# Attention chunks on quarter arrays for every unit, and weight sums in buffers of their own, stored one set late in program order

## The chip, the cores and the metric

The kernel runs on one core of one Trainium2 chip. The metric is the device time of one execution, in microseconds (us). Engine names are those of the profile: PE is TensorE's matmuls and PEld its weight loads, DVE is VectorE, ACT ScalarE, POOL GpSimd, SP SyncE (which here issues every DMA).

## What is computed

Chunked attention, whose output goes through a gated two-layer network, all in float32:

```python
# q, k, v: (8, 8, 576, 64); chunks of 64 along the sequence, 9 of them per (batch, head)
scores = (q_c @ k_c.T) / 8                     # 64 x 64 per chunk
attn   = softmax(scores, axis=-1)
x      = (attn @ v_c)                          # laid out as (4608 tokens, 512)
out    = (sigmoid(x @ w_gate) * (x @ w_val)) @ w_out      # 512 -> 1536 -> 512
```

The three weight matrices reach the chip as 64-bit floats and are rebuilt there as a high and a low part. Each large product takes three passes (high x high, high x low, low x high).

## The kernel before

**Blocks, steps, units.** The tokens are cut into nine blocks of 512 (`m`), the 1536 hidden columns into twelve slices of 128 (`f`). Blocks 0 to 2 take a plain path: a step (`m`, `f`) is 24 matmuls `up` (L315), a sigmoid and a product on ACT and DVE, and 12 matmuls `down` (L341) into four accumulators. Blocks 3 to 8 go in three pairs (`n`) through a Strassen-like scheme: seven products `cx`, `cy`, `cz` (L475) of combined inputs `xc` with combined weights `wr`, then `acc` (L550). Attention is cut into 36 units of 16 chunks, four units for each block; two neighbouring units are a pair.

**Weights.** In the first block, twelve slices of weights are loaded (`load_weights`, L110), rebuilt on ACT and DVE (`convert_weights`, L131 to L139) and used at once. During blocks 1 and 2 the kernel stores in DRAM what the Strassen part will read back: copies of the weights (`keep_given` L378, `keep_outer` L383) and 24 sets of weight sums made on POOL (`keep_sums` L392 to L402). The Strassen part loads them with `load_group` (L419, L422) and `load_outer` (L436); the first two groups are asked for in block 2, after step 8.

**Buffers of a set of sums.** `a_val` and `a_sum` come from the two buffers `ob`, through which the output rows of a block also go on their way to DRAM (`evacuate`); `a_both` is one buffer, `spare`, which held the last raw weights before.

**Attention.** Units 0 to 7 go one by one: `products` (L177) against a block-diagonal `kbd`, softmax, four transposes on PE (L222), two half-height copies into the block-diagonal `pbd` (L225 and L227 or L229), and `values` (L238). These matmuls contract over 128 rows and have 64 output rows. Units 8 to 35 go in pairs through `tiled_products` (L271) and `tiled_values` (L286), 32 matmuls of 64x64x64 each, on quarters of the array; their transposes are done on DVE (L614) into alternating halves of `pbd`.

**Order.** START and MIDDLE are lists written by hand: L loads a unit, S or s makes its scores, E its softmax, T or t its transposes, A its values, W loads and C converts weights, H is an `up`, D a `down`. What belongs to START the scheduler orders by itself; from MIDDLE on PE keeps program order, and in `rest()` (blocks 1 to 8) PE and DVE do. SP's queue is ordered by the scheduler throughout. In `rest()`, attention is fed between the matmuls by a credit counter (`tick`, `insert`); the attention loop is `flow`.

Of the kernel before, what the change touches and what calls it, by code (L numbers as in the profile page):

```python
# [29 lines left out]
L0 L1 V0 W0o S0 s1 V1 E0 W0u t0 C0.0 E1 L2 t1 L3 C0.1 A0 A1 W1u S2 C0.2 s3 C1.0 H0.0a E2 W1o E3 C1.1  # L30
T2 W2u T3 D V3 L4 V2 C2.0 A2 C1.2 A3 L5 H0.1a H0.0b W3o D W3u C2.1 C3.0 H0.1b D s4 W4u W2o H0.2 C3.2
C2.2 W4o C3.1 C4.0 D W5u E4 C4.1 C5.0 C5.1 H0.3 D s5 C4.2 t4 E5 W6u H0.4 D W7u C6.0 V5 W6o C7.0 C6.1
# [3 lines left out]
C9.0 W8o C8.2 W9o C9.1 W10u A4 A5 H0.8 W10o D C10.0 C9.2 C10.2 W11u H0.9 C10.1 D H0.10 C11.0 C11.1 D  # L36
W11o H0.11 S7 V7 S6 D L9 E6 H1.0a C11.2 D V6 E7 T6 T7 D H1.1a A6 A7 D H1.0b L8 V8 H1.1b V9 D
# [5 lines left out]

FIRST_TILED = 8
# [6 lines left out]
def chunk_attn_moe(ctx: ExitStack, tc: tile.TileContext, q, k, v, w, out):  # L51
# [17 lines left out]
    early = xp.tile([P, 4, 8, D], F32, tag="x", name="early")  # L69
    zeros = early[:, 0, 0].bitcast(mybir.dt.bfloat16)  # L70
# [4 lines left out]
    pbd = [pbd2[:, i] for i in range(2)]  # L75
    for i in range(2):
        eng = nc.gpsimd if i else nc.vector
        eng.memset(kbd[i][0:D, :, 1, :], 0.0)
        eng.memset(kbd[i][D:P, :, 0, :], 0.0)
# [63 lines left out]
    state, both = {}, {}  # L143
    xt, raw = {}, {}

    def load(j):
        m, h, u = units[j]
        g = 2 * m + h
        qt = ap2.tile([P, 2, 256], F32, name="qt")
        kb = kbd[j % 2]  # L150
        nc.sync.dma_start(qt, q[g, u].rearrange("p (a n) -> p a n", a=2))
        if j >= FIRST_TILED:
            kt = kb[:, :, 0, :]
            nc.sync.dma_start(kt, k[g, u].rearrange("p (a n) -> p a n", a=2))
            state[j] = dict(qt=qt, kt=kt)
            return
        for i in range(2):
            s = slice(i * D, (i + 1) * D)
            nc.sync.dma_start(kb[s, :, i, :], k[g, u, s].rearrange("p (a n) -> p a n", a=2))
        state[j] = dict(qt=qt, kb=kb)  # L160
# [6 lines left out]

    def products(j):  # L170
        s = state[j]
        sc = ps_a.tile([P, 512], F32, tag="psa", name="sc")
        for a in range(2):
            for t in range(2):
                for c in ((0, 1), (1, 0))[a * t]:
                    n0 = (2 * t + c) * D
                    nc.tensor.matmul(  # L177
                        sc[c * D:(c + 1) * D, (2 * a + t) * P:(2 * a + t + 1) * P],
                        lhsT=s["qt"][:, a, n0:n0 + D], rhs=s["kb"][:, a, :, n0:n0 + D],
                        start=True, stop=True,  # L180
                    )
        return sc.rearrange("p (g k) -> p g k", k=D)

    def scores(j, on_scalar=False):
        s = state[j]
        scv = products(j)
        mx = sm.tile([P, 8], F32, name="mx")
        nc.vector.reduce_max(out=mx, in_=scv, axis=AX.X)
        if j < 4:
            pr = early[:, j]  # L190
        else:
            if j // 2 not in both:
                both[j // 2] = ap2.tile([P, 2, 8, D], F32, name="pr", bufs=1)
            pr = both[j // 2][:, j % 2]
        s["pr"] = pr
        if not on_scalar:
            nc.vector.tensor_tensor(out=pr, in0=scv, in1=mx.unsqueeze(2).broadcast_to([P, 8, D]), op=ALU.subtract)
            return
        nc.vector.tensor_scalar_mul(out=mx, in0=mx, scalar1=-0.125)
        sums = s["sums"] = sm.tile([P, 8], F32, name="sums")  # L200
        for i in range(8):
            nc.scalar.activation(
                pr[:, i], scv[:, i], AF.Exp, scale=0.125, bias=mx[:, i:i + 1], accum_out=sums[:, i:i + 1])

    def softmax(j):
        pr = state[j]["pr"]
        if "sums" not in state[j]:
            nc.scalar.activation(pr, pr, AF.Exp, scale=0.125)
            sums = sm.tile([P, 8], F32, name="sums")
            nc.vector.reduce_sum(out=sums, in_=pr, axis=AX.X)  # L210
        else:
            sums = state[j]["sums"]
        nc.vector.tensor_scalar_add(out=sums, in0=sums, scalar1=1e-9)
        inv = sm.tile([P, 8], F32, name="inv")
        nc.vector.reciprocal(out=inv, in_=sums)
        nc.vector.tensor_tensor(out=pr, in0=pr, in1=inv.unsqueeze(2).broadcast_to([P, 8, D]), op=ALU.mult)

    def transposes(j, on_scalar=False):
        pr = state[j]["pr"].rearrange("p (x h) k -> p x (h k)", h=2)
        tp = ps_a.tile([P, 512], F32, tag="psa", name="tp")  # L220
        for i in range(4):
            nc.tensor.transpose(tp[:, i * P:(i + 1) * P], pr[:, i, :], ident)  # L222
        tv = tp.rearrange("p (x q) -> p x q", q=D)
        pb = pbd[j % 2]
        nc.scalar.copy(pb[0:D, :, 0, :], tv[0:D])  # L225
        if not on_scalar:
            nc.vector.tensor_copy(pb[D:P, :, 1, :], tv[D:P])  # L227
        else:
            nc.scalar.copy(pb[D:P, :, 1, :], tv[D:P])  # L229

    def values(j):
        m, h, u = units[j]
        s = state.pop(j)
        pb = pbd[j % 2]
        av = ps_a.tile([P, 512], F32, tag="psa", name="av")
        for c in range(4):
            for a in ((0, 1), (1, 0))[c == 3]:
                nc.tensor.matmul(  # L238
                    av[a * D:(a + 1) * D, c * P:(c + 1) * P],
                    lhsT=s["vt"][:, a, c, :], rhs=pb[:, 4 * a + c, :, :],  # L240
                    start=True, stop=True,
                )
        avv = av.rearrange("p (c h q) -> p h c q", h=2, q=D)
        if m >= FIRST_PAIR:
            n, half = divmod(m - FIRST_PAIR, 2)
            if (n, u) not in raw:
                raw[n, u] = xp.tile([P, 2, 2, TB], F32, tag="x", name="raw")
            dst = raw[n, u][:, :, half, h * 256:(h + 1) * 256]
            nc.scalar.copy(dst.rearrange("p h (c q) -> p h c q", q=D), avv)
            return  # L250
        if h == 0:
            xt[m, u] = xp.tile([P, 2, 2, TB], F32R, tag="x", name="xt")
        x = xt[m, u]
        hi = x[:, 0, :, h * 256:(h + 1) * 256].rearrange("p h (c q) -> p h c q", q=D)
        lo = x[:, 1, :, h * 256:(h + 1) * 256].rearrange("p h (c q) -> p h c q", q=D)
        nc.scalar.copy(hi, avv)  # L256
        nc.vector.tensor_tensor(out=lo, in0=avv, in1=hi.bitcast(F32), op=ALU.subtract)


    def tiled_products(j):  # L260
        sc = [ps_a.tile([P, 512], F32, tag="psa", name="sc") for _ in range(2)]
# [14 lines left out]
    def tiled_values(j, pt):  # L276
        m, h, _ = units[j]
        av = [ps_a.tile([P, 512], F32, tag="psa", name="av") for _ in range(2)]
# [11 lines left out]
        for u in range(2):  # L290
            if m >= FIRST_PAIR:
                n, half = divmod(m - FIRST_PAIR, 2)
                if (n, u) not in raw:
                    raw[n, u] = xp.tile([P, 2, 2, TB], F32, tag="x", name="raw")
            elif h == 0:
                xt[m, u] = xp.tile([P, 2, 2, TB], F32R, tag="x", name="xt")
            for i in range(2):
                src = av[i][:, u * 256:(u + 1) * 256]
                if m >= FIRST_PAIR:
                    nc.scalar.copy(raw[n, u][:, i, half, cols], src)  # L300
                else:
                    hi, lo = (xt[m, u][:, part, i, cols] for part in range(2))
                    nc.scalar.copy(hi, src)
                    nc.vector.tensor_tensor(out=lo, in0=src, in1=hi.bitcast(F32), op=ALU.subtract)
# [140 lines left out]
    def operands(n):  # L445


        low = None
        for i, (name, (u, b), less) in enumerate(MADE):
            at = raw[n, u][:, :, b]  # L450
            if less:
                (u0, b0), (u1, b1) = less
                yield 1.2
# [344 lines left out]
```

## Time and profile before

| | |
|---|---|
| median of 3 runs | 944.46 us (941.83 to 946.08) |
| profiled execution: its own time | 945.38 us |
| profiled execution: span | 943.6 us |
| mean granted TensorE clock | 0.983 |
| busy: PE, PEld, DVE, ACT, POOL | 911.6, 746.7, 604.2, 343.5, 141.7 us |
| DMA | 189.71 MB, mean 201 GB/s |

The profiled execution lasted 1.8 us longer than its span, and 0.9 us longer than the median run. Busy times are unions of intervals on one engine. A granted clock of 1.0 is 2.4 GHz and one of 0.5 is 1.2 GHz; a value between them over a stretch is a mixture of both.

### The profile page before, as it was taken

The numbers are of one execution on the slowest core, as the hardware profiler recorded it, in microseconds if no ns is written. First come the engines' busy times: TensorE is split into PE (matmuls) and PEld (weight loads), VectorE is DVE, ScalarE is ACT, GpSimd is POOL, SyncE is SP. The second block draws the span as 40 slices with busy tenths as digits, with TensorE's granted clock in tenths as the row PEclk, the third lists the DMA queues.
The fourth block names the chain that finished last, engine by engine and source line by source line (L and its number), as shares of the span: only waits on it lengthen the run. The fifth ranks groups of instructions, "written<-read, shape, count | busy, mean of one in ns | idle before, by whom it ended". The sixth has DMA issues, their size and how long they took to land.

```text
span 943.6 us, 14868 instructions
## 1 busy us (share of the span) xinstructions
PE 911.6 (97%) x5856; PEld 746.7 (79%) x5856; DVE 604.2 (64%) x1003; ACT 343.5 (36%) x586; POOL 141.7 (15%) x204
## 2 busy tenths in 40 slices
PE   6899999999999996999999999999999999999998
PEld 4777879888888885788887788888877888888886
DVE  6889875566677664777768675777686335445332
ACT  5989644223234341132342433323324221121222
POOL 1000003990059991000000000000000000000000
PEclk7999999999999997999999999999999999999999
DMA  8788886343143438566575857666565565656661
GB/s 274 236 283 288 282 300 210 131 135 109 53 135 112 135 112 302 188 221 228 189 257 207 283 182 245 199 241 209 198 222 205 186 216 177 205 183 215 221 223 45
DMA packets 80837, 189.71 MB, mean 201 GB/s; under 512 B 7040, under 2 KB 37760, under 8 KB 76160
## 3 DMA queue, kind: packets, MB, share of 16 engines
q1 hardware_dynamic: 80768, 188.77, 58.9%
q8 instruction: 46, 0.75, 0.3%
q14 instruction: 23, 0.19, 0.1%
HBM read 150.99 MB, written 37.75 MB: 200 GB/s over the span
## 4 chain that ended last, share of the span: by engine, by line
PE 73%; DMA 9%; POOL 7%; ACT 4%; DVE 4%; issue 1%; SPq 1%; POOLq 0%; DVEq 0%; ACTq 0%
PE acc L550 19%; PE cy L475 16%; PE cz L475 11%; PE cx L475 11%; PE g L315 9%; PE acc L341 5%; DMA w_raw<-w_in 4%; POOL a_sum L398 2%; POOL a_both L401 2%; POOL a_val L392 2%; DMA sums<-a_both 2%; PE sc L271 1%; PE av L286 1%; POOL a_both L400 1%; DMA wr<-sums 1%
## 5 line engine op out<-in xcount | busy, mean ns | idle before, releaser
L315 PE MATMUL g<-xt,w 128*128 128x512 f32 (+1 forms) x960 | 209.6, 374 | 8.5 <-ACT w L138 3.6
L315 PEld LDWEIGHTS g<-xt,w 128*128 128x128 f32 x960 | 169.4, 191 | 42.7 <-ACT hf L324 3.9
L550 PE MATMUL acc<-wr,hh 128*128 128x512 f32 x576 | 178.0, 390 | 0.0
L475 PE MATMUL cy<-xc,wr 128*128 128x512 f32 x648 | 159.2, 390 | 0.9 <-DVE u L493 0.9
L475 PEld LDWEIGHTS cy<-xc,wr 128*128 128x128 f32 x648 | 121.6, 188 | 26.5 <-DVE u L493 1.3
L550 PEld LDWEIGHTS acc<-wr,hh 128*128 128x128 f32 x576 | 107.9, 188 | 22.4
L475 PE MATMUL cz<-xc,wr 128*128 128x512 f32 x432 | 107.5, 395 | 8.5 <-DMA wr<-sums 8.5
L550 PE MATMUL acc<-wr,hl 128*128 128x512 f32 x288 | 112.7, 391 | 2.9 <-DVE hl L542 2.9
L475 PE MATMUL cx<-xc,wr 128*128 128x512 f32 x432 | 106.1, 391 | 0.0
L475 PEld LDWEIGHTS cz<-xc,wr 128*128 128x128 f32 x432 | 81.4, 190 | 25.9 <-issue 8.9
L614 DVE STREAM_TRANSPOSE pbd<-pr 32x256 f32<-32x256 f32 x224 | 97.6, 436 | 3.9
L542 DVE TENSOR_TENSOR hl<-hid,hh 128x512 fp32r<-128x512 f32 x72 | 49.5, 689 | 76.9 <-ACT hh L540 76.3
L475 PEld LDWEIGHTS cx<-xc,wr 128*128 128x128 f32 x432 | 80.7, 188 | 16.9
L341 PE MATMUL acc<-w,hh 128*128 128x512 f32 x288 | 92.5, 403 | 0.0
L540 ACT CAST hh<-hid 128x512 fp32r<-128x512 f32 x72 | 44.8, 622 | 125.3 <-PE acc L550 102.0
L392 POOL TENSOR_TENSOR a_val<-w 128x256 f32<-128x256 f32 x48 | 38.2, 814 | 206.4 <-DMA out<-ob 204.8
L550 PEld LDWEIGHTS acc<-wr,hl 128*128 128x128 f32 x288 | 54.1, 188 | 16.1 <-DVE hl L542 5.0
L341 PEld LDWEIGHTS acc<-w,hh 128*128 128x128 f32 x288 | 54.0, 192 | 11.6 <-ACT xt L256 0.2
L493 DVE TENSOR_TENSOR u<-cy,s 128x512 f32<-128x512 f32 x36 | 24.8, 688 | 58.2 <-PE cy L475 48.0
L326 DVE TENSOR_TENSOR hf<-g,hf 128x512 f32<-128x512 f32 (+1 forms) x40 | 25.4, 636 | 50.9 <-PE g L315 44.4
L341 PE MATMUL acc<-w,hl 128*128 128x512 f32 x144 | 57.4, 398 | 0.0
L510 DVE TENSOR_TENSOR u<-cy,s 128x512 f32<-128x512 f32 x36 | 24.9, 691 | 46.0 <-PE cy L475 45.9
(109 smaller groups left out, 978.4 us busy)
## 6 DMA issues: line engine op xcount, KB each, us to landing
wr<-sums SPq DMA_DIRECT2D x72, 512.0 KB, 4.6
wr<-outer SPq DMA_DIRECT2D x36, 1024.0 KB, 4.8
w_raw<-w_in SPq DMA_DIRECT2D x36, 512.0 KB, 5.3
wr<-given SPq DMA_DIRECT2D x36, 512.0 KB, 3.7
sums<-a_both SPq DMA_DIRECT2D x24, 512.0 KB, 3.5
qt<-q_in SPq DMA_DIRECT2D x36, 256.0 KB, 4.6
vt<-v_in SPq DMA_DIRECT2D x36, 256.0 KB, 4.4
given<-w SPq DMA_DIRECT2D x36, 256.0 KB, 4.9
```

Source lines behind the costliest of these rows:

```text
L315: nc.tensor.matmul(ps[:, tok], lhsT=wt[f, which][:, wpart, c:c + P], rhs=x[:, part, i, tok], start=n == 0, stop=n == 11)
L326: nc.vector.tensor_tensor(out=hf, in0=pv, in1=hf, op=ALU.mult)
L341: nc.tensor.matmul(acc[m, t], lhsT=hx[:, ts], rhs=wt[f, 2][:, wpart], start=f == 0 and i == 0, stop=f == NF - 1 and i == 2,)
L392: nc.gpsimd.tensor_tensor(out=val[:, 2 * n:2 * n + 2], in0=parts[:, 0], in1=parts[:, 1], op=ALU.add)
L398: nc.gpsimd.tensor_tensor(out=o, in0=x, in1=y, op=op)
L475: nc.tensor.matmul(bank, lhsT=lhs(wpart, c), rhs=x[:, part, c], start=start and k == 0, stop=stop and k == 5, skip_group_check=True)
L493: nc.vector.tensor_tensor(out=u2, in0=y, in1=s1, op=ALU.add)
L510: nc.vector.tensor_tensor(out=u3, in0=y, in1=s1, op=ALU.add)
L540: nc.scalar.copy(hh, h)
L542: nc.vector.tensor_tensor(out=hl, in0=h, in1=hh.bitcast(F32), op=ALU.subtract)
L550: nc.tensor.matmul(acc[m, t], lhsT=hx[:, ts], rhs=wo[f][:, wpart], start=f == 0 and i == 0, stop=f == NF - 1 and i == 2)
L614: nc.vector.transpose(out=pb[dst, :, c, i, :], in_=ps[src, 8 * h:8 * (h + 1), k, :])
```

## The change

All attention units go in pairs over quarter arrays; `products`, `values`, `scores`, `softmax` and `transposes` work on a pair, and `kbd` and `pbd` with their memsets are gone. A pair's transposed scores lie in `pt`, one buffer. For the second pair the scores, and for the first pair the transposes, use accumulator banks of PSUM (`bank`, `aside`). The sums of a set are made in place in a buffer of their own (`sb`), `a_both` alternates between `spare` and a buffer of its own, and the store of a set is issued when the next set has been made. Sets are spread as 1, 1, 2 over three steps through blocks 1 and 2. In `rest()`, SP is put in program order as PE and DVE are.

```diff
-L0 L1 V0 W0o S0 s1 V1 E0 W0u t0 C0.0 E1 L2 t1 L3 C0.1 A0 A1 W1u S2 C0.2 s3 C1.0 H0.0a E2 W1o E3 C1.1
-T2 W2u T3 D V3 L4 V2 C2.0 A2 C1.2 A3 L5 H0.1a ...
+L0 L1 V0 W0o S0 s1 V1 E0 W0u C0.0 E1 L2 t0 t1 L3 C0.1 A0 W1u S2 C0.2 s3 C1.0 H0.0a E2 W1o E3 C1.1
+T2 W2u T3 D V3 L4 V2 C2.0 A2 C1.2 L5 H0.1a ...
...
-    xp = ctx.enter_context(tc.tile_pool(name="xp", bufs=4))
+    xp = ctx.enter_context(tc.tile_pool(name="xp", bufs=2))
+    sb = ctx.enter_context(tc.tile_pool(name="sb", bufs=1))
...
-    kbd = [const.tile([P, 2, 2, 256], F32, name=f"kbd{i}") for i in range(2)]
-    pbd2 = const.tile([P, 2, 8, 2, D], F32, name="pbd")
...
-    for i in range(2):
-        nc.gpsimd.memset(pbd[i][0:D, :, 1, :], 0.0)
-        nc.gpsimd.memset(pbd[i][D:P, :, 0, :], 0.0)
...
     def load(j):
-        kb = kbd[j % 2]
-        nc.sync.dma_start(qt, q[g, u].rearrange("p (a n) -> p a n", a=2))
-        for i in range(2):
-            s = slice(i * D, (i + 1) * D)
-            nc.sync.dma_start(kb[s, :, i, :], k[g, u, s].rearrange("p (a n) -> p a n", a=2))
+        for name, src in (("qt", q), ("kt", k)):
+            t = state[j][name] = ap2.tile([P, 2, 256], F32, name=name)
+            nc.sync.dma_start(t, src[2 * m + h, u].rearrange("p (a n) -> p a n", a=2))
...
+    def bank(name, aside=False):
+        if aside:
+            return ps_o.tile([P, 512], F32, tag="acc", name=name)
+        return ps_a.tile([P, 512], F32, tag="psa", name=name)
+
+    def products(j, aside=False):
+        sc = [bank("sc", aside) for _ in range(2)]
         for u in range(2):
             s = state[j + u]
...
     def scores(j, on_scalar=False):
+        n, i = divmod(j, 2)
+        if n not in pairs:
+            pr = early[:, n] if n < 2 else ap2.tile([P, 8, 2, D], F32, name="pr", bufs=1)
+            pairs[n] = dict(sc=products(2 * n, n == 1), pr=pr, sums={})
...
+    def turned():
+        return ap2.tile([P, 2, 2, 4, D], F32, name="pt", bufs=1)
...
     def transposes(j, on_scalar=False):
+        n, u = divmod(j, 2)
+        s = pairs[n]
+        if u == 0:
+            s["pt"] = turned()
+        tp = bank("tp", n == 0)
+        for g in range(4):
+            nc.tensor.transpose(tp[:, g * P:(g + 1) * P], s["pr"][:, 4 * u + g].rearrange("p i k -> p (i k)"), ident)
+        pt = s["pt"][:, u].rearrange("p a c q -> p (a c q)")
+        if on_scalar:
+            nc.scalar.copy(pt, tp)
+        else:
+            nc.vector.tensor_copy(pt, tp)
...
     def keep_sums(p, which, c):
-        val = mp.tile([P, 4, P], F32, tag="ob", name="a_val")
+        val = sb.tile([P, 4, P], F32, name="a_val")
...
-        sm4 = mp.tile([P, 4, P], F32, tag="ob", name="a_sum")
+        for o, x, y, op in ((3, 2, 3, ALU.add), (2, 0, 2, ALU.subtract), (0, 3, 0, ALU.subtract), (1, 1, 0, ALU.subtract)):
+            nc.gpsimd.tensor_tensor(out=val[:, o], in0=val[:, x], in1=val[:, y], op=op)
+        if c == 0:
+            both = wp.tile([P, 4, 2, P], F32R, tag="spare", name="a_both")
+        else:
+            both = sb.tile([P, 4, 2, P], F32R, name="a_both")
...
-        nc.sync.dma_start(
-            sums[p, which][:, :, c], both.rearrange("p s a n -> p s (a n)").bitcast(F32))
+        return sums[p, which][:, :, c], both.rearrange("p s a n -> p s (a n)").bitcast(F32)
...
-        for t, g, s in ((one, 2, slice(0, 2)), (two, 1, slice(2, 4))):
+        for t, g, s in ((one, 2, slice(0, 4, 3)), (two, 1, slice(1, 3))):
...
-            kept = pr, pbd2[:, j // 2 % 2].rearrange("p (u a c) h q -> p u a (c h) q", u=2, a=2)
+            kept = pr, turned()
...
+    made = []
     def keep(n):
         for _ in range(n):
...
-                keep_sums(p, which, c)
+                made.append(keep_sums(p, which, c))
+            if len(made) > 1 or made and not kept:
+                nc.sync.dma_start(*made.pop(0))
...
-                    keep(1)
-                else:
-                    keep(2)
+                keep(2 if f % 3 == 2 else 1)
+                if m == 2:
                     if f == 8:
                         for which in range(2):
                             load_group(0, 0, which)
...
-        with tc.manual_schedule(engines={mybir.EngineType.DVE}):
+        with tc.manual_schedule(engines={mybir.EngineType.DVE, mybir.EngineType.SP}):
             rest()
```

## Rows read from the trace of the kernel before

**Rows 1.** The page's 40 slices of the span (23.6 us each): granted PE clock, in tenths.

```profile
PEclk7999999999999997999999999999999999999999
```

**Rows 2.** Busy us of the engines in three stretches, granted clock, DMA share, GB/s.

```profile
25.00:45.00 20.00, 15.85 (x126) 13.87 (x125) 17.36 (x37) 19.92 (x47) 0.00 (x0) 0.91 0.71 217
38.00:141.50 103.50, 99.60 (x533) 80.65 (x529) 86.93 (x162) 77.10 (x158) 0.00 (x0) 0.98 0.87 285
141.50:361.70 220.20, 220.18 (x1806) 182.12 (x1802) 143.97 (x237) 77.14 (x117) 137.85 (x192) 1.00 0.39 128
```

**Rows 3.** Waits, whole span: us in total, times, longest us.

```profile
POOL a_val L392 <- DMA out<-ob: 204.8, 2, 151.2
...
PE cz L475 <- DMA wr<-sums: 8.5, 1, 8.5
...
PE g L315 <- ACT hf L324: 2.9, 2, 2.3
```

**Rows 4.** Timeline of POOL, SP's queue and DVE: start us, us, work, idle before.

```profile
269.17 1.99 POOL L392 TENSOR_TENSOR a_val<-w 128x256 f32<-128x256 f32 x2 [53.59 <-DMA out<-ob]
...
356.12 2.15 POOL L401 TENSOR_TENSOR a_both<-a_sum,a_both 128x512 fp32r<-128x512 f32 x1
...
358.30 0.52 SPq L402 DMA_DIRECT2D sums<-a_both  x1
...
361.22 0.59 SPq L422 DMA_DIRECT2D wr<-sums  x1
...
362.78 2.35 DVE L465 TENSOR_TENSOR xc<-raw,xc 128x1024 fp32r<-128x1024 f32 x2
```

**Rows 5.** The chain that ended last, in order: start us, us, work.

```profile
45.01 7.20 DMA w_raw<-w_in
...
61.43 7.35 PE g L315 x24
...
131.16 4.11 DMA w_raw<-w_in
...
174.48 5.44 PE g L315 x24
...
188.08 2.72 PE acc L341 x12
...
362.33 7.76 DMA wr<-sums
370.23 2.90 PE cz L475 x6
373.13 4.33 PE acc L341 x12
...
442.41 1.36 PE cy L475 x6
```

**Rows 6.** Timeline of PE: the products of two units, both ways.

```profile
140.07 1.97 PE L177 MATMUL sc<-kbd,qt 128*64 128x128 f32 x32
...
171.73 1.16 PE L271 MATMUL sc<-kbd,qt 64*64 64x64 f32 x64
```

**Rows 7.** SP's queue, the first and the last stores of weight copies before block 1.

```profile
41.98 0.94 SPq L378 DMA_DIRECT2D given<-w  x2
...
147.43 0.59 SPq L378 DMA_DIRECT2D given<-w  x1
```

**Rows 8.** DMA issues: count, KB each, median us to landing.

```profile
given<-w SPq DMA_DIRECT2D x36, 256.0 KB, 4.9
...
outer<-w SPq DMA_DIRECT2D x12, 512.0 KB, 5.3
```

**Rows 9.** ACT's copies of transposed scores: busy us, mean ns.

```profile
L225 ACT COPY pbd<-tp 64x512 f32<-64x512 f32 x8 | 4.5, 577 | 2.8 <-PE tp L222 2.8
```

**Rows 10.** Groups of DVE's `hl`: 217 to 268 us (POOL idle), then 270 to 357.

```profile
L330 DVE TENSOR_TENSOR hl<-hf,hh 128x512 fp32r<-128x512 f32 x6 | 4.2, 692 | 4.1 <-ACT hh L328 4.1
L330 DVE TENSOR_TENSOR hl<-hf,hh 128x512 fp32r<-128x512 f32 x10 | 9.7, 972 | 7.3 <-ACT hh L328 7.3
```

More of the change, by code (lines that the diff above doesn't have):

```diff
@@ L67, in chunk_attn_moe @@
     ident = const.tile([P, P], F32, name="ident")
-    early = xp.tile([P, 4, 8, D], F32, tag="x", name="early")
-    zeros = early[:, 0, 0].bitcast(mybir.dt.bfloat16)
+    early = xp.tile([P, 2, 8, 2, D], F32, tag="x", name="early")
+    zeros = early[:, 0, 0, 0].bitcast(mybir.dt.bfloat16)
     nc.vector.memset(zeros, 0.0)
-    kbd = [const.tile([P, 2, 2, 256], F32, name=f"kbd{i}") for i in range(2)]
-    pbd2 = const.tile([P, 2, 8, 2, D], F32, name="pbd")
-    pbd = [pbd2[:, i] for i in range(2)]
-    for i in range(2):
-        eng = nc.gpsimd if i else nc.vector
-        eng.memset(kbd[i][0:D, :, 1, :], 0.0)
-        eng.memset(kbd[i][D:P, :, 0, :], 0.0)
-    for i in range(2):
-        nc.gpsimd.memset(pbd[i][0:D, :, 1, :], 0.0)
-        nc.gpsimd.memset(pbd[i][D:P, :, 0, :], 0.0)
     make_identity(nc, ident)
@@ L142, in chunk_attn_moe @@
     units = [(m, h, u) for m in range(NB) for h in range(2) for u in range(2)]
-    state, both = {}, {}
+    state = {}
     xt, raw = {}, {}
@@ L166, in load_values @@
         state[j]["vt"] = vt
[L170 to L190, printed above, removed]
-        else:
[L192 to L257, printed above, removed]
@@ L274, in tiled_products, with scores @@
         return [x.rearrange("p (g k) -> p g k", k=D) for x in sc]
-    def tiled_values(j, pt):
+    pairs = {}
+    def scores(j, on_scalar=False):
+        n, i = divmod(j, 2)
[3 more added lines that the diff above has]
+        s = pairs[n]
+        scv, pr = s["sc"][i], s["pr"][:, :, i]
+        mx = sm.tile([P, 8], F32, name="mx")
+        nc.vector.reduce_max(out=mx, in_=scv, axis=AX.X)
+        if not on_scalar:
+            nc.vector.tensor_tensor(out=pr, in0=scv, in1=mx.unsqueeze(2).broadcast_to([P, 8, D]), op=ALU.subtract)
+            return
+        nc.vector.tensor_scalar_mul(out=mx, in0=mx, scalar1=-0.125)
+        sums = s["sums"][i] = sm.tile([P, 8], F32, name="sums")
+        for g in range(8):
+            nc.scalar.activation(
+                pr[:, g], scv[:, g], AF.Exp, scale=0.125, bias=mx[:, g:g + 1], accum_out=sums[:, g:g + 1])
@@ new lines, in softmax @@
+    def softmax(j):
+        n, i = divmod(j, 2)
+        pr = pairs[n]["pr"][:, :, i]
+        sums = pairs[n]["sums"].get(i)
+        if sums is None:
+            nc.scalar.activation(pr, pr, AF.Exp, scale=0.125)
+            sums = sm.tile([P, 8], F32, name="sums")
+            nc.vector.reduce_sum(out=sums, in_=pr, axis=AX.X)
+        nc.vector.tensor_scalar_add(out=sums, in0=sums, scalar1=1e-9)
+        inv = sm.tile([P, 8], F32, name="inv")
+        nc.vector.reciprocal(out=inv, in_=sums)
+        nc.vector.tensor_tensor(out=pr, in0=pr, in1=inv.unsqueeze(2).broadcast_to([P, 8, D]), op=ALU.mult)
@@ new lines, in turned, with transposes @@
+    def turned():
+        return ap2.tile([P, 2, 2, 4, D], F32, name="pt", bufs=1)
+    def transposes(j, on_scalar=False):
+        n, u = divmod(j, 2)
+        s = pairs[n]
+        if u == 0:
[8 more added lines that the diff above has]
+            nc.vector.tensor_copy(pt, tp)
@@ L277, in tiled_values, with values @@
+    def values(j, pt):
         m, h, _ = units[j]
-        av = [ps_a.tile([P, 512], F32, tag="psa", name="av") for _ in range(2)]
+        av = [bank("av") for _ in range(2)]
         vt = [state.pop(j + u)["vt"] for u in range(2)]
@@ L289, in tiled_values @@
         cols = slice(h * 256, (h + 1) * 256)
-        for u in range(2):
-            if m >= FIRST_PAIR:
[L292 to L304, printed above, removed]
+        n, half = divmod(m - FIRST_PAIR, 2)
+        if m >= FIRST_PAIR:
+            if n not in raw:
+                raw[n] = xp.tile([P, 2, 2, 2, TB], F32, tag="x", name="raw")
+        elif h == 0:
+            xt[m] = xp.tile([P, 2, 2, 2, TB], F32R, tag="x", name="xt")
+        for i in range(2):
+            src = av[i].rearrange("p (u n) -> p u n", u=2)
+            if m >= FIRST_PAIR:
+                nc.scalar.copy(raw[n][:, :, i, half, cols], src)
+            else:
+                hi, lo = (xt[m][:, :, part, i, cols] for part in range(2))
+                nc.scalar.copy(hi, src)
+                nc.vector.tensor_tensor(out=lo, in0=src, in1=hi.bitcast(F32), op=ALU.subtract)
     def up(m, f, which, tok):
@@ L310, in up @@
         for u in range(2):
-            x = xt[m, u]
+            x = xt[m][:, u]
             for i in range(2):
@@ L392, in keep_sums @@
             nc.gpsimd.tensor_tensor(out=val[:, 2 * n:2 * n + 2], in0=parts[:, 0], in1=parts[:, 1], op=ALU.add)
[L393 to L403 removed]
+        for o, x, y, op in ((3, 2, 3, ALU.add), (2, 0, 2, ALU.subtract), (0, 3, 0, ALU.subtract), (1, 1, 0, ALU.subtract)):
+            nc.gpsimd.tensor_tensor(out=val[:, o], in0=val[:, x], in1=val[:, y], op=op)
+        if c == 0:
+            both = wp.tile([P, 4, 2, P], F32R, tag="spare", name="a_both")
+        else:
+            both = sb.tile([P, 4, 2, P], F32R, name="a_both")
+        nc.gpsimd.tensor_copy(both[:, :, 0], val)
+        nc.gpsimd.tensor_tensor(out=both[:, :, 1], in0=val, in1=both[:, :, 0].bitcast(F32), op=ALU.subtract)
+        return sums[p, which][:, :, c], both.rearrange("p s a n -> p s (a n)").bitcast(F32)
     places = [0]
@@ L430, in load_group @@
             1: (of_given(one, 0), "B11"), 2: (of_given(one, 1), "B21"), 6: (of_sums(one, 2), "T2"),
-            5: (of_sums(one, 3), "T1"), 4: (of_given(two, 0), "T4"), 7: (of_sums(two, 1), "T3"),
-            3: (of_sums(two, 2), "B22")}
+            5: (of_sums(one, 3), "T1"), 4: (of_given(two, 0), "T4"), 3: (of_sums(two, 1), "B22"),
+            7: (of_sums(two, 2), "T3")}
     def load_outer(p):
@@ L449, in operands @@
         for i, (name, (u, b), less) in enumerate(MADE):
-            at = raw[n, u][:, :, b]
+            at = raw[n][:, u, :, b]
             if less:
@@ L453, in operands @@
                 yield 1.2
-                nc.vector.tensor_tensor(out=at, in0=raw[n, u0][:, :, b0], in1=raw[n, u1][:, :, b1], op=ALU.subtract)
+                nc.vector.tensor_tensor(out=at, in0=raw[n][:, u0, :, b0], in1=raw[n][:, u1, :, b1], op=ALU.subtract)
             t = wp.tile([P, 2, 2, TB], F32R, tag=f"u{i}", name="xc")
@@ L564, in flow @@
                 yield "S"
-                scv = tiled_products(j)
+                scv = products(j)
                 if j + 2 < 4 * NB:
@@ L582, in flow @@
                 yield "A"
-                tiled_values(j - 2, kept[1])
+                values(j - 2, kept[1])
                 if more:
@@ L671, in run @@
         elif what == "A":
-            values(int(arg))
+            values(int(arg), pairs.pop(int(arg) // 2)["pt"])
         elif what == "W":
@@ L682, in run @@
             finish()
-    for op in START.split():
-        run(op)
     kept = [(p, which, c) for p in range(6) for which in range(2) for c in range(2)]
+    made = []
     def keep(n):
@@ L693, in keep @@
                     keep_given(p, which)
-                keep_sums(p, which, c)
+                made.append(keep_sums(p, which, c))
+            if len(made) > 1 or made and not kept:
+                nc.sync.dma_start(*made.pop(0))
+    for op in START.split():
+        run(op)
     def rest():
```

30 lines of the change are left out of this document (5 added, 25 removed).

## The prediction

> **What bounds the kernel now.** Read the slices of the page first: PE has 0.9 or more of its full clock from the second slice on, except in slice 16, around 354 to 377 us [rows 1]. The busy times by stretch say how full it is: 99.60 of 103.50 us from 38 to 141.5, and 220.18 of 220.20 from there to 361.7 [rows 2]. So the kernel is bound by PE almost everywhere, and two places are left where something else sets the time: the one hole at 361.7, and the first 141 us.
>
> The hole is explained by three views together. The waits give its size and what ended it: PE's first product `cz` of the Strassen part waited 8.5 us for a load of weight sums [rows 3]. The timeline shows why that load was late: POOL began its last fourteen sets only at 269.17, after 53.59 us of idleness behind stores of output rows, finished at 358.27, SP sent the last store at 358.30, and the load of sums that `cz` needs went out behind it, at 361.22 [rows 4]. In all POOL sat 204.8 us waiting for `out<-ob`, in two waits [rows 3]: the sums share the `ob` buffers with the rows that leave the chip. The chain of waits shows that the hole costs more than its own length: the six matmuls of `cz` behind it take 2.90 us against 1.36 later, the twelve of `acc` 4.33 against 2.72 [rows 5], at a granted clock that the page shows fallen to 0.7 for that slice [rows 1], between the 1.2 and 2.4 GHz levels.
>
> In the first stretch the same chain does not run along PE: it runs through loads of raw weights, six long pieces from 45.01 to 131.16 (7.20 us the first, 4.11 the last) [rows 5], and the conversions behind them. There DMA is 87% busy and PE still nearly full [rows 2]: two limits close together. And from 25 to 45 us ACT is busy 19.92 of 20 us while PE has 15.85 [rows 2].
>
> **The transition, minus 11.6 us.** The sums get buffers of their own, so no set waits for output rows any more. The fourteen sets of block 2 took 358.27 - 269.17 = 89.1 us, 6.4 us a set [rows 4]. The new spacing asks for four sets in three steps. A step is 24 `up` matmuls, 5.44 us, and 12 `down`, 2.72 [rows 5]; three steps and the two attention pieces of a pair (1.16 each, like the last row of [rows 6]) make 26.8 us, 6.7 a set. POOL keeps that pace, just. Its first `a_both` waits for `spare`, so for the last raw weights, whose load ends at 135.3 [rows 5], and their conversion; the last set is made in step 7 of block 2, four steps or over 30 us before the Strassen part begins. The loads of the first group are then held only by the weight slots that they overwrite, those of steps 8 to 11; `cz` needs the first slot alone. So SP no longer holds anything back and the wait goes: 8.5 us, and with it the cold matmuls, (2.90 - 1.36) + (4.33 - 2.72) = 3.1.
>
> What is late next? DVE's last two `xc` end at 365.1 [rows 4], the hole having covered them. Without it PE runs `cz` and the last `down` until 361.7 + 1.36 + 2.72 = 365.8, the first `cx` to 367.1, and only then wants a late `xc`: a margin of 2 us or more. I take the whole 11.6; if the cover fails, some 3 us come back.
>
> **Work taken from PE in blocks 0 and 1, minus 4.1 us.** The products of a pair take 1.97 us the old way and 1.16 the new way [rows 6], 0.81 less; the values do the same arithmetic at the same shapes and I take the same. Eight such pieces change. Three lie in the first 38 us, where PE waits; five lie behind: 5 x 0.81 = 4.05. The transposes stay as many. The Trainium skill (TensorE: Matmul & The Clock Gate, section "Back-to-back issue gap") puts a floor of about 25 ns under a matmul of 64 columns or fewer, and so speaks against cutting 128 columns to 64. By that floor, as an estimate, 64 records would need 1.6 us, the five pieces would give 1.9 us, and the time would be 927. The row disagrees: 64 of them ended within 1.16 us, 18 ns each [rows 6].
>
> **DMA order, minus 2.9 us.** This part is in no line about attention. Before, the scheduler moved stores of weight copies ahead: the first went out at 41.98 us, and they continue to 147.43 [rows 7], 36 of 256 KB for `given` and 12 of 512 KB for `outer` in all [rows 8], 15.7 MB between the weight loads that the chain runs through. In program order every store of `rest()` stands behind the loads of units 10 and 11, which wait for PE's products of units 8 and 9, in block 1. So the first 141 us lose that traffic. What they can give back at most is PE's idleness there, 103.50 - 99.60 = 3.9 [rows 2], and the cold matmuls behind one stall, 7.35 against 5.44 us [rows 5], 1.9, together 5.8. Of the stalls 2.9 us were waits for ACT's sigmoid behind other ACT work [rows 3], which fewer stores don't cure. I take half, 2.9; bounds 0 and 5.8.
>
> The stores fall into blocks 1 and 2 instead, where DMA was 39% busy [rows 2], so they hide there. Queued behind a store are loads of `q`, `k` and `v`, wanted a pair later, some 27 us; a store waits only for a set made one set earlier.
>
> **The first 38 us, minus 1.1 us.** ACT loses four copies there: the two half copies of t0 and of t1 become one each, and those of T2 and T3 move to DVE, which copies full height in place of half. At 577 ns [rows 9] that is 2.3 us of an engine that is full from 25 to 45 [rows 2]. Against it, unit 0 now waits for unit 1's load and products before its softmax, and the transposes for both softmaxes. Nothing in the trace shows that start; bounds are a gain of 4 us (ACT's copies and the cheaper cold products) and a loss of 4 (a unit's chain laid behind another's). I take half of ACT's copies.
>
> **At nothing.** The memsets ran while the first loads were on their way. `pt` has one buffer where `pbd` had two: its writers on DVE come behind operations that need later matmuls than the values that read it, so they find it free. Loads of sums in two pieces of 2 KB per partition in place of one of 4 KB are issued a whole group ahead, as before. Fewer ACT copies per pair in later blocks fall under a full PE.
>
> **Sum.** 11.6 + 4.1 + 2.9 + 1.1 = 19.7. The profiled execution was 945.4, so 925.7 by it; the median of the runs is 0.9 lower, so 925.
>
> **Rivals.**
> - *Weights pace block 0* (0.20). The conversions on ACT and DVE stay as they are: DVE is busy 86.93 of 103.50 us and ACT 77.10 [rows 2]. If they and the loads set the end of the block, PE's saved work returns as waits and only the transition counts: 944.5 - 11.6 = 933. For it: the chain. Against: the stores leave.
> - *Block 0 opens fully* (0.15): all 5.8, and 4 at the start: 944.5 - 11.6 - 4.1 - 5.8 - 4 = 919.
> - *The transition stalls on something else* (0.07), a late `xc` or a slot: 3 to 8 us back, 928 to 933; with the first rival up to 940.
> - *Quarter products are dearer in block 0 than the row* (0.04): no more than 4.1 lost, 929.
> - *SP blocked by POOL: slower* (0.03). In program order each store waits for POOL and holds loads behind it. From about 163 us (PE's products of units 8 and 9, at 171.7 before [rows 6], less 8) the stores go at POOL's pace. Losing the 8 us of the other parts, the old hole's 8.5 and its cold 3.1 needs the last store some 19.6 us after PE is ready at 361.7 - 8 = 353.7, less 8.5 for the loads, thus at 365, or (365 - 163) / 24 = 8.4 us a set. I read 6.4 with `spare` alone, and two buffers can only help. At 9 us a set it would be 24 x 0.6 = 14 us slower, 958.
> - *POOL beside the conversions: no gain* (0.04). DVE's `hl` takes 692 ns with POOL idle and 972 in the mean with POOL busy [rows 10]. If the sums ran from 45 us on, with ten such operations a step at that excess of 0.28 us, block 0 would need 11 x 2.8 = 31 us more of DVE, 118 us in the 103.5 [rows 2]: 14 us back, 939 or, with the first rival, 945. Waiting for `spare` excludes it, except for the first set. The Trainium skill (SBUF — State Buffer, section "Who interferes with whom") states the rule: a DVE instruction with two SBUF inputs contends with a GpSimd instruction that reads SBUF; the two rows agree with it.
>
> **Chances and range.** The forecast holds 0.47. Range: the second rival less 2 us for the spread of runs, 917, to the first plus 3, 936; outside it are parts of the third, fifth and sixth. Half a per cent is 4.7 us, about what a measurement of this kernel can tell from no change: slower takes the fifth rival and 0.01 of unforeseen order in START, 0.04; the same takes most of the sixth and the tail of the third, 0.05; faster 0.91.
>
> **What would show it.** PE without a wait at the first `cz`, whose six matmuls take 1.4 us; a granted clock of 9 tenths in every slice but the first; POOL starting near 140 and ending before step 8 of block 2; no `given` store before block 1, and PE's products of units 8 and 9 some 8 us before 171.7; the Strassen part as long as before: from the first `cz` to the end 943.6 - 370.2 = 573.4 us, less the cold 3.1. Wrong, if SP waits for POOL with loads behind it, or if the Strassen part itself changes length.

## The result, and the profile after

The changed kernel takes 928.66 us (median of 4 runs, 927.61 to 929.69) against 945.17 for the kernel before beside it (4 runs, 941.83 to 946.08): ratio 0.9832, 95% interval 0.9803 to 0.986. Measured again later, 4 runs of it gave 929.41 (928.08 to 930.22) against 941.38 for the kernel before beside them (7 runs, 939.65 to 944.0): the gain is 16.5 us in the first measurement and 12.0 in the second. The profiled execution took 929.69 us, its span is 927.9 (before: 943.6).

The page's slices (23.2 us each) for POOL and the granted clock, to be read beside [rows 1]: slice 16 no longer shows the lower clock, and POOL has finished before it.

```profile
POOL 0100031277889800000000000000000000000000
...
PEclk9999999999999999999999999999999999999999
```

The three stretches of [rows 2]:

```profile
25.00:45.00 20.00, 14.21 (x138) 12.00 (x139) 19.44 (x41) 19.91 (x46) 2.21 (x5) 0.91 0.72 250
38.00:141.50 103.50, 100.70 (x696) 83.41 (x697) 86.21 (x157) 77.39 (x153) 10.34 (x14) 0.97 0.42 140
141.50:361.70 220.20, 219.87 (x1830) 181.58 (x1829) 141.37 (x234) 74.86 (x103) 121.44 (x173) 1.00 0.61 208
```

The DMA share from 38 to 141.5 us fell from 0.87 to 0.42 and rose after it from 0.39 to 0.61: the stores moved. PE's busy time there hardly rose, and ACT is as full from 25 to 45 us as before.

The waits of the whole span (line, released by: us in total, times, longest us) no longer have `cz` or `out<-ob` of [rows 3]. POOL now waits for `spare`, which the last raw weights hold (here `w_val`), and for its own stores:

```profile
POOL a_both L344 <- DVE w_val L125: 102.8, 1, 102.8
...
POOL a_both L344 <- DMA sums<-a_both: 47.8, 6, 36.3
...
PE tp L213 <- DVE early L201: 12.9, 2, 10.1
...
PE g L258 <- ACT hf L267: 3.5, 2, 2.3
```

And the timeline of SP, POOL and PE where [rows 4] and [rows 5] had the hole:

```profile
171.14 2.73 SPq L321 DMA_DIRECT2D given<-w  x3
173.97 0.72 SPq L639 DMA_DIRECT2D sums<-a_both  x1
...
130.31 0.61 POOL L344 CAST a_both<-a_val 128x512 fp32r<-128x512 f32 x1 [102.79 <-DVE w_val L125]
...
179.20 0.61 POOL L344 CAST a_both<-a_val 128x512 fp32r<-128x512 f32 x1 [36.33 <-DMA sums<-a_both]
...
323.07 1.21 SPq L639 DMA_DIRECT2D sums<-a_both  x2
328.70 0.33 SPq L362 DMA_DIRECT2D wr<-given  x1
...
357.03 1.52 PE L418 MATMUL cz<-xc,wr 128*128 128x512 f32 x6
```

The last sums are stored at 323, five us before the first group is loaded, and `cz` starts at 357.03 without a wait.

**Where the 15.7 us of span came from.** Set the same events of both traces side by side. PE's products of units 8 and 9 begin at 167.24 (before 171.73): 4.5 us. From there to the moment when `cz` could have started, PE needed 190.0 us before (370.23 less the wait of 8.55) and 189.8 after: 0.2. The hole itself: 8.55. From the start of `cz` to the first `cx`, 7.07 us before and 4.08 after: 3.0 of cold matmuls (granted clock 0.56 there before). The Strassen part is otherwise unchanged, and lost 0.5. So the transition gave 11.5 us, and everything ahead of it 4.5, where 8.1 was forecast. The way from the products of units 8 and 9 to `cz` is 189.8 us in each of the five traces of the changed kernel and of its variants in START, so the first figure is firm. The start of block 1 differs by some 2 us between traces of one kernel, so the second is known to no better than that; of the later measurement, with its smaller gain, there is no trace of the kernel before.

### The profile page after: what moved, and what is told of

Read it like the earlier page. It is cut to its first block, busy times and chain, and to the rows that moved or that the text cites. A ratio compares the mean times of both kernels' runs of the same rounds, so it can differ in the third digit from the quotient of the medians.

```text
span 927.9 us, 15296 instructions
## 1 busy us (share of the span) xinstructions
PE 898.7 (97%) x6112; PEld 737.9 (80%) x6112; DVE 599.0 (65%) x997; ACT 340.5 (37%) x552; POOL 136.5 (15%) x198
## 4 chain that ended last, share of the span: by engine, by line
PE 92%; DVE 4%; ACT 2%; issue 1%; DMA 1%; SPq 0%; DVEq 0%; ACTq 0%
PE g L258 21%; PE acc L493 20%; PE cy L418 16%; PE cz L418 11%; PE cx L418 11%; PE acc L284 10%; PE sc L165 2%; PE av L230 2%; PE tp L213 1%; DMA kt<-k_in 0%; DVE w_raw L123 0%; DVE hl L485 0%; ACT w_raw L120 0%; DMA vt<-v_in 0%; DVE w_raw L125 0%
## 5 line engine op out<-in xcount | busy, mean ns | idle before, releaser
L258 PE MATMUL g<-xt,w 128*128 128x512 f32 (+1 forms) x960 | 206.9, 371 | 5.3 <-ACT hf L267 3.5
L557 DVE STREAM_TRANSPOSE pt<-pr 32x256 f32<-32x256 f32 x224 | 97.7, 436 | 4.0
L493 PEld LDWEIGHTS acc<-wr,hl 128*128 128x128 f32 x288 | 54.0, 188 | 16.5 <-DVE hl L485 5.4
L433 ACT COPY s<-cx 128x512 f32<-128x512 f32 x36 | 21.2, 590 | 78.0 <-PE cx L418 77.3
```

The source lines that it names most:

```text
L258: nc.tensor.matmul(ps[:, tok], lhsT=wt[f, which][:, wpart, c:c + P], rhs=x[:, part, i, tok], start=n == 0, stop=n == 11)
L433: nc.scalar.copy(s1, x)
L493: nc.tensor.matmul(acc[m, t], lhsT=hx[:, ts], rhs=wo[f][:, wpart], start=f == 0 and i == 0, stop=f == NF - 1 and i == 2)
L557: nc.vector.transpose(out=pb[dst, :, c, i, :], in_=ps[src, 8 * h:8 * (h + 1), k, :])
```

## The experiments

In each, two milestones are read from the trace: when block 1 starts (PE's first 256-wide `up`; before 144.82, changed kernel 140.41) and how long PE needs from the products of units 8 and 9 to the first `cz` (before 198.5, changed kernel 189.8). The runs without an interval are one execution each. The kernel before, run 7 times beside each set, took 942.8 us (939.8 to 945.93) beside runs 1, 2, 3 and 5, 943.24 (940.5 to 947.88) beside 4, 6, 7 and 8, and 941.38 beside 9, 10 and 11.

**1. Without program order on SP.**

```diff
-with tc.manual_schedule(engines={mybir.EngineType.DVE, mybir.EngineType.SP}):
+with tc.manual_schedule(engines={mybir.EngineType.DVE}):
```

> The changed kernel, with SP in rest() ordered by the scheduler again (quarter products and sum buffers stay). Theory (DMA order is worth something in block 0): the stores of weight copies go back between the weight loads of the first 141 us, so PE's products of units 8 and 9 start 1 to 3 us after the 167.2 us of the changed kernel, and the whole takes 929 to 932. Rival (block 0 does not feel those stores, its gain came from cheaper products alone): products of units 8 and 9 within 0.5 us of 167.2, time as the changed kernel's, 928 to 929.

997.42 us: some 55 us slower than before, which neither expectation allowed for. SP's queue (start, us, work) shows six and then five stores in a row, some 5 us apart, the pace of POOL, with loads of `kt` between:

```profile
199.21 30.92 SPq L639 DMA_DIRECT2D sums<-a_both  x6
...
230.84 0.95 SPq L140 DMA_DIRECT2D kt<-k_in  x1
...
235.25 24.20 SPq L639 DMA_DIRECT2D sums<-a_both  x5
```

PE's waits from 140 to 400 us:

```profile
PE sc L165 <- DMA kt<-k_in: 31.2, 4, 17.6
PE acc L284 <- ACT hh L271: 26.0, 1, 26.0
```

With buffers of their own, the scheduler put stores ahead of loads and output rows (ACT, whose `hh` PE waits for here, itself stood 31.6 us for output rows). Without the order the buffers are a loss. Block 1 starts at 143.81, 3.4 us later than with the order.

**2. Program order and quarter arrays, but sums in `ob`, stored at once, spaced as before.**

```diff
-        val = sb.tile([P, 4, P], F32, name="a_val")
+        val = mp.tile([P, 4, P], F32, tag="ob", name="a_val")
...
-                made.append(keep_sums(p, which, c))
+                keep_sums(p, which, c)
```

> The changed kernel with the sums made in the ob buffers again, one a_both, stored at once, spaced 1 and 2 a step as before (quarter products and SP's program order stay). Theory (the hole was POOL waiting for output rows): the wait of the first cz returns with 8 to 9 us and the cold matmuls with 3, so 940. Rival (SP's program order alone had removed it): no wait at the first cz, 929. A third possibility: with stores at once in program order SP waits for POOL in front of loads, and the time is over 945.

939.08 us. Block 1 starts at 140.17, as with the change. No wait at `cz`, but 199.9 us lie between the products of units 8 and 9 and `cz`: PE waits 3.2 us for `vt` and 2.2 for `kt`, queued behind stores that wait for POOL, with cold matmuls behind. So the time is the 940 of the theory, but by other waits than the one it named. Own buffers, the late store and the spacing together are worth 10 us here; no run separates the three.

**3. Program order alone**, on the kernel before.

> The kernel before with one edit: SP in program order in rest(). Theory: the weight loads lose the traffic of the stores, so PE's products of units 8 and 9 start 1 to 3 us before their 171.7, and the hole at the first cz stays or grows, since POOL still waits for output rows: 942 to 946. Rival: 171.7 stays within 0.5 us.

937.65 us, below the 942 that was expected at the least. Block 1 starts at 139.41: the order alone brings the whole gain of block 0. The wait at `cz` falls to 0.78, but PE waits 5.9 us for loads behind stores (166 to 345 us):

```profile
PE sc L271 <- DMA kbd<-k_in: 3.0, 2, 2.1
PE av L286 <- DMA vt<-v_in: 2.9, 1, 2.9
```

So it is 198.8 us to `cz`: the wait was moved, not removed.

**4. Quarter arrays alone**: SP ordered by the scheduler, sums in `ob`.

> The kernel before with the quarter products alone: SP ordered by the scheduler, sums in the ob buffers, one a_both, stored at once, spaced as before. Theory (the cheaper products give block 0 next to nothing, its gain came from the order of the stores): block 1 begins 0 to 1.5 us before the 144.8 us of the kernel before, the hole at the first cz is there with 8 us and more: 943 to 946. Rival (the products are worth their 4 us, and program order costs some of it): block 1 begins at 140 to 141.5, 939 to 941.

944.9 us, block 1 at 144.35 and a wait of 9.47 at `cz`: the kernel before, for all that can be measured. With this run four kernels form a square, in which only the order and the products (with the START that they need) differ. The first 256-wide `up` of block 1, start and us, before, in this run, in run 3 and in run 2:

```profile
144.82 3.04 PE L315 MATMUL g<-xt,w 128*128 128x256 f32 x24
144.35 3.04 PE L258 MATMUL g<-xt,w 128*128 128x256 f32 x24
139.41 3.04 PE L315 MATMUL g<-xt,w 128*128 128x256 f32 x24
140.17 3.04 PE L258 MATMUL g<-xt,w 128*128 128x256 f32 x24
```

The order is worth 5.4 us with the old products and 4.2 with the new ones; the new products are worth 0.5 without the order and -0.8 with it, which is less than two traces of one kernel differ by.

**5. Unit 1's scores without their exponentials in START** (`S1` for `s1`), because PE in the changed kernel waits 12.9 us for the first softmax.

> The changed kernel with one letter of START changed: unit 1's scores in capital S, so its maximum is subtracted on DVE and one exponential of 512 columns on ACT takes the place of eight of 64 with their sums. Theory (the first pair's two softmaxes, one behind the other, are what block 0 lost at its start): ACT loses some 1.8 us there, the first transposes come 1 to 2 us before 17.8 us, and block 0 ends 1 to 2 us sooner: 926.5 to 927.5. Rival (the conversions of the first weights set the first product of block 0, not the softmax): first transposes sooner, block 0 within 0.5 us, 928.5.

929.59 us (927.78 to 931.32), ratio 0.9868 (0.9843 to 0.9893). The wait for the softmax falls from 12.9 to 9.0 us, a wait for ACT's `hh` (L271) grows from 0.9 to 2.4, and block 1 still starts at 140.02. So PE's wait for the first softmax is not what sets the moment, 52 us, at which the first 512-wide `up` begins.

**6. The same for unit 4** (`S4` for `s4`), because its eight exponentials stand on ACT ahead of a sigmoid.

> The changed kernel with unit 4's scores in capital S in START: its eight exponentials on ACT (57.35 to 59.6 us, with a table load before and after) become one, made later in E4, so nothing but conversions stands ahead of the sigmoid of step 2. Theory (in block 0 the cheaper products were eaten by PE's wait of 2.3 us for that sigmoid and the cold matmuls behind it, some 1.6): the wait goes, block 1 begins 2 to 4 us before 140.4, and the time is 924.5 to 926.5. Rival (ACT and DVE as a whole set block 0's pace, the wait only shows it): another wait of the same size appears within the next steps, block 1 begins within 1 us of 140.4, 928 to 929.

926.64 us (926.48 to 927.18), ratio 0.9826 (0.9785 to 0.9867). PE's wait for the sigmoid is 0.95 instead of 2.3, and the 24 matmuls behind it take 5.75 instead of 7.18. Only the wait can be put down to the edit: in run 11, the changed kernel itself, these matmuls take 5.74.

**7. Two sets in every step.**

```diff
-                keep(2 if f % 3 == 2 else 1)
+                keep(2)
```

> The changed kernel with two sets of sums asked for in every step, so all 24 by step 1 of block 2. It prices the rival that SP, in program order, waits for POOL in front of loads: POOL needs about 6 us a set, 12 a double step, where a step with its share of attention takes 9, so stores fall behind and loads of q, k and v behind them come late. Theory: PE waits for kt or vt in block 1, 10 to 35 us in all with the cold matmuls, 938 to 965. Rival (loads are a pair ahead and absorb it): 928 to 931.

947.8 us, some 19 us slower than the changed kernel and no faster than the one before. What is lost is one wait of PE and the slow matmuls behind it. SP's queue and the PE instruction it stops:

```profile
271.16 4.82 SPq L639 DMA_DIRECT2D sums<-a_both  x2
276.07 1.57 SPq L145 DMA_DIRECT2D vt<-v_in  x2
277.73 5.61 SPq L305 DMA_DIRECT2D out<-ob  x4
...
282.55 1.22 PE L284 MATMUL acc<-w,hh 128*128 128x512 f32 x2 [17.71 <-DVE ob L304]
```

The output rows of block 1 stand behind stores that wait for POOL, which makes a set in 5.65 us; DVE can't free the accumulators, and PE stops. The place is the rows, not the loads of `q`, `k`, `v` that the prediction had named.

**8. The same work on POOL, spread through the conversions too.** As soon as both slices of a pair are converted, four further sets are made into the `sb` buffers as `keep_sums` does, and never stored: work that the output doesn't need.

```diff
             convert_weights(int(f), int(part))
...
+                if all((2 * p + i, x) in turned_up for i in range(2) for x in range(2)):
+                    for which in range(2):
+                        for c in range(2):
+                            idle_sums(p, which, c)
```

> The changed kernel with 24 extra sets of weight sums made on POOL in block 0, each as soon as its weights are converted, and thrown away (nothing is stored of them; the real sets are made later as before). It measures what POOL beside the conversions costs. By the rival of the prediction (two-input operations of DVE slowed by some 0.28 us each) block 0 gets up to 14 us longer: block 1 begins at 150 to 155, 938 to 943. Theory that DVE has room there (86.2 us busy of 103.5): block 1 begins within 2 us of 140.4, 928 to 931.

978.58 us, far above both expectations; block 1 starts at 189.59, 49 us late. The same groups of DVE's instructions (busy us, mean ns), first of this kernel from 61.5 to 165, then of the changed kernel from 61.5 to 140:

```profile
L128 DVE TENSOR_TENSOR w<-w_raw,w 128x512 fp32r<-128x512 f32 x16 | 16.5, 1047 | 0.1
...
L122 DVE TENSOR_SCALAR w_raw<-w_raw 128x512 uint32<-128x512 uint32 x14 | 12.2, 876 | 1.2 <-ACT w_raw L120 1.2
L273 DVE TENSOR_TENSOR hl<-hf,hh 128x512 fp32r<-128x512 f32 x7 | 9.4, 1343 | 1.5 <-ACT hh L271 1.5
...
L269 DVE TENSOR_TENSOR hf<-g,hf 128x512 f32<-128x512 f32 x7 | 4.8, 679 | 1.3 <-PE g L258 1.3
```

```profile
L128 DVE TENSOR_TENSOR w<-w_raw,w 128x512 fp32r<-128x512 f32 x14 | 9.4, 683 | 0.7 <-ACT w L127 0.7
L273 DVE TENSOR_TENSOR hl<-hf,hh 128x512 fp32r<-128x512 f32 x10 | 8.1, 813 | 2.0 <-ACT hh L271 1.9
...
L269 DVE TENSOR_TENSOR hf<-g,hf 128x512 f32<-128x512 f32 x10 | 6.8, 685 | 4.9 <-PE g L258 4.9
...
L122 DVE TENSOR_SCALAR w_raw<-w_raw 128x512 uint32<-128x512 uint32 x10 | 4.2, 419 | 2.6 <-ACT w_raw L120 2.6
```

Every conversion on DVE slows, those with one input too; of the instructions on 512 columns, only those that read a matmul's result (here `g`) keep their time. That POOL waits for `spare` until 130 us in the changed kernel is therefore part of what makes it work.

**9. The old products with own sums and order.** On the kernel before: SP in order, sums made in place in the half of `kbd` that is idle after unit 7, one `a_both`, stored a set late, spaced 1, 1, 2.

```diff
-        val = mp.tile([P, 4, P], F32, tag="ob", name="a_val")
+        val = kbd[c][:, :, 1, :].rearrange("p a (h n) -> p a h n", h=2)
...
```

> The kernel before with its block-diagonal products for the first eight units, but with SyncE in program order and with sums that no longer use the buffers of the output rows: a set is made in place in the idle halves of the block-diagonal key buffer (two instructions of POOL more a set for the split layout), a_both is the one spare buffer, a set is stored when the next one has been made, and sets come 1, 1, 2 over three steps. So it has the two edits that the runs so far credit, without the quarter arrays. Theory: quarter products gave block 0 nothing and are worth only the space that they free, so block 1 starts near 139.5 as with the order alone, the first cz waits under 1 us, no load of a unit is late by more than 3 us, and the time is 926 to 930, as the changed kernel or better. Rival A: quarter products are worth their forecast 4 us, hidden so far by the order of START: block 1 at 143 or later and 932. Rival B: one a_both is too few, since POOL waits for every store: the last set ends later than 350, cz waits again, and the time is 934 or more.

932.38 us (930.35 to 933.96), ratio 0.9897 (0.9872 to 0.9922): above the range that my theory gave. But block 1 starts at 139.96, so rival A is not why. Of rival B the cause is there, not the place: POOL waited for stores of its one `a_both` (49.7 us in 8 waits), so its sets came late, SP stood for them, and behind it the output rows:

```profile
259.40 0.51 SPq L698 DMA_DIRECT2D sums<-a_both  x1
260.01 1.56 SPq L165 DMA_DIRECT2D vt<-v_in  x2
261.67 5.77 SPq L362 DMA_DIRECT2D out<-ob  x4
...
265.88 0.69 DVE L361 COPY ob<-acc 128x512 f32<-128x512 f32 x1 [8.00 <-DMA out<-ob]
...
273.63 3.06 PE L315 MATMUL g<-xt,w 128*128 128x512 f32 x12 [2.28 <-DVE hf L326]
```

DVE waited 8.00 us for output rows, was late with the softmax behind them, and PE waited 2.28. From the products of units 8 and 9 to `cz` it needs 192.4 us, 2.6 more than the changed kernel; the time is 3.0 longer than run 11's. `cz` starts without a wait. The transition works with the old products.

**10 and 11. Both START edits together, and the changed kernel again,** beside run 9.

> The changed kernel with the scores of unit 1 and of unit 4 placed in START without their eight exponentials (the exponentials then go with the softmax operations that follow), so both edits tried singly are together. Singly the first left block 0 as it was (140.02 against 140.41) and the second took 2 us (138.35). Theory: the first 52 us are paced by the conversions on ACT and DVE, so the two together give what the second gives alone: block 1 at 138 to 138.7, 926 to 927. Rival: the second edit left ACT a gap that the first can now use: block 1 at 137 or earlier, 925 or less.

> The changed kernel as it is, beside the two others of this call on the same chip, so that differences of 2 us can be read against it: 927.5 to 930, first cz without a wait.

926.26 us (926.09 to 927.37), ratio 0.9837 (0.9814 to 0.986), against 929.41 (928.08 to 930.22), ratio 0.9865 (0.9845 to 0.9886). Run 10 agrees with run 6: the two runs of the version with `S4` lie at 926.1 to 927.4, three measurements without it at 927.6 to 931.3. That is the best version found, some 3 us better than the change. Block 1 starts at 137.01 in run 10; but the unchanged kernel of run 11 shows 138.59 where its first trace had 140.41, so this milestone of one trace does not carry 2 us. The times do, but where in the trace the 3 us lie is not shown.

## Why the prediction was right, and where it was off

925 was forecast and 928.66 measured, inside the range; as a gain, 19.4 us were forecast and 16.5 and 12.0 measured. The direction and the largest term held; three smaller terms, 8.1 us together, gave 4.5. That it was not less is in part luck: one of the three failed, and another, sized too small, made up for some of it.

**The transition, 11.6 forecast, 11.5 measured.** Each step can be seen: no wait for output rows, POOL done by 321 us, loads no longer behind it, no late `xc` in place of the hole. But the prediction put it down to buffers and spacing, and gave the order no part in it. Runs 1 to 3 show that it takes both edits: buffers without order end some 55 us behind the kernel before, order without buffers leaves 198.8 us to `cz`. The step "SP no longer holds anything back" is nearly so: SP stands 13 us in nine waits for POOL, the longest 4.3, and PE does not feel it. In run 7, where the same stores are asked for more densely, PE does. How much of this the late store does, and how much the buffers, is not shown.

**Work taken from PE in blocks 0 and 1, 4.1 forecast.** This step failed. With program order, block 1 starts at 139.41 and 139.96 with the old products (runs 3 and 9) and at 138.05 to 140.41 with the new ones in the same START (the changed kernel, runs 2, 7 and 11); without it, at 144.82 (before), 144.35 and 143.81 (new products, runs 4 and 1). The instructions did get cheaper, but the time came back in two places. First, every kernel but that of run 8 reaches its first 512-wide `up` at 51 to 53 us, whatever PE did before. ACT is busy 19.91 of 20 us from 25 to 45 and is the likely cause, but no run made ACT faster there by more than the traces differ. Second, PE's chain from 51 us, of run 3 and of the changed kernel:

```profile
51.94 0.58 PE sc L177 x6
52.52 5.71 PE g L315 x24
58.23 1.36 PE acc L341 x6
59.59 1.02 PE sc L177 x16
60.61 2.49 PE g L315 x10
```

```profile
51.35 1.09 PE sc L165 x64
52.44 5.68 PE g L258 x24
...
58.14 1.68 ACT pr L187 x11
...
59.84 1.28 ACT L267
...
61.14 0.60 ACT hf L267
...
61.79 7.18 PE g L258 x24
```

With the old products a piece of one unit (1.02 us) lay between the two steps. The new products come as a whole pair, ahead of the first step; the gap behind is empty, and PE waits for unit 4's exponentials and the sigmoid on ACT, then runs cold: 7.18 us for 24 matmuls. The missing piece is not all of the wait: ACT's sigmoid itself ends at 61.74 here and at 61.20 in run 11, but at 59.99 in run 3, and why the pairs bring it later is not shown. From the second step on the saving is seen: to block 1 78.8 us in runs 3 and 9, 77.3 in run 11, about two pieces of 0.81. The prediction counted five such pieces as lying on the path and did not ask what filled PE while ACT was late.

**DMA order, 2.9 forecast with bounds 0 and 5.8.** Mis-sized: run 3 shows 144.82 - 139.41 = 5.4, near the upper bound, and run 2 beside run 4 shows 144.35 - 140.17 = 4.2. The first `given` store goes out at 171.14, as foreseen. PE has no wait from 52 to 166 us in run 3; I had left the waits for the sigmoid out of the gain, but in run 3 these go too. That it is the stores' traffic fits the loads of raw weights, which land in a median of 4.5 us in run 3 and 5.3 before. But stores also stood in SP's queue ahead of such loads (9.6 us in seven waits for DVE's conversions, L383, from 30 to 170 us before), and no run separates the two.

**The first 38 us, 1.1 forecast.** Not seen. The first transposes come at 17.84 where they came at 12.38, behind both units' softmax, and the first 512-wide `up` came no earlier (52.37 us, before 51.17); run 5 shows that curing part of this moves nothing.

**The rivals.** *Weights pace block 0* may hold up to 52 us; behind it PE has no wait for weights, nor in run 3 any wait at all until 166 us. *SP blocked by POOL* did not happen, but its mechanism is real (runs 1, 2, 7): at a denser spacing its place is the output rows, and PE loses 17.7 us in one wait, where the prediction had priced a late last store. *POOL beside the conversions* was priced at 14 us (with the first rival 933 + 14 is 947, not the 945 that stands there) and measured at 49 in run 8: I took one operation's excess, 0.28 us, for ten a step; measured, `hl` grew by 0.53 us and a conversion with one input by 0.46. The Trainium skill (SBUF — State Buffer, section "Who interferes with whom") lists `tensor_scalar` among the operations that can, if their operands allow it, take the port pair that DVE shares with GpSimd, and says that an instruction with two SBUF inputs contends with GpSimd's reads. The 419 ns that became 876 agree, and so does `hf`, with one input outside SBUF, at 685 and 679.

**What would show it.** The clock, the missing wait at `cz`, the stores and the end of POOL came out as written. The Strassen part, from `cz` to the end, took 570.9 us against 573.4 - 3.1 = 570.3. POOL did start near 140 (130.31), but after two sets stood 36.3 us for a store queued behind loads for units 10 and 11. Units 8 and 9 came 4.5 us earlier, not 8.

What stays open: why the same kernel starts block 1 at 140.41 in one trace and 138.59 in another. The wait for the sigmoid was 2.32 and 1.89 us, and the 24 matmuls behind it took 7.18 and 5.74; that is the difference, but not its cause. The length of the wait alone does not decide it: in run 5 PE waited 2.92 us there, and the matmuls took 5.75.

## What to carry to other kernels

A store that waits for a compute engine holds everything behind it in its queue, loads and output rows alike; here, moving such work off the critical path took buffers of its own and a fixed place in the queue, late enough that the data is there. When work is taken from a busy engine, look at what its idle gaps would have been without that work: a piece that covered another engine's lateness saves nothing when it goes. And order alone, with no instruction changed, can be the larger part of what a change to the arithmetic seems to bring: try each edit with and without the other before crediting either.

## What the runs showed of the hardware

In run 8, with POOL busy 96.3 of 103.5 us, DVE's one-input conversion of 128x512 (L122) took 876 ns in place of 419 and the two-input `hl` 1343 in place of 813; DVE's `hf`, which reads the matmul's result, stayed at 0.68 us.

Of two executions of the same kernel, PE's wait of 2.32 us was followed by 7 us at a granted clock of 0.78, that of 1.89 us by 7 us at 1.00: the first lies between the two levels, 1.2 and 2.4 GHz, the second at the upper one. In run 5, 7 us at 1.00 followed a wait of 2.92 us.
